# Attention and two gated layers on one core: the second layer's weight sums on VectorE, the sums of its activations earlier and in a block of their own

## The chip, the cores and the metric

One core of a Trainium2 chip runs one program: attention for 2 x 12 heads, then two feed-forward layers with two matrix products each. The metric is the device time of one execution in microseconds. Before the change the median of three runs is 565.75 us (563.14 to 567.88).

## The reference, cut to what matters

```python
attn_out = _attn_ref(q, k, v, cap)          # 2 x 12 heads, 448 tokens, 64 wide; tanh cap, softmax
x = attn_out as (896 tokens, 768)
def _moe_ref(x, w_gate, w_val, w_out, rms_g):   # 768 -> 1536 -> 768
    xn = x / sqrt(mean(x * x) + 1e-6) * rms_g
    g, val = xn @ w_gate, xn @ w_val
    return (silu(g) * val) @ w_out
def _moe2_ref(x, w_in, w_out, alpha):           # 768 -> 2048 -> 768
    h = x @ w_in
    return (maximum(h, 0) + alpha * minimum(h, 0)) @ w_out
```

Everything is float32. The "second layer" of this document is the second product of the first block, the one with `moe_w_out` (1536 to 768).

## The kernel before, in words

After the attention all matrix products are written with seven block products in place of eight (Strassen's scheme in Winograd's form): weights and activations are cut in 2 x 2 blocks, sums and differences of blocks are multiplied, and the products are added up again. The sums of weight blocks are S1 to S4 (S1 = A21 + A22, S2 = S1 - A11, S3 = A22 - S2, S4 = A12 - S2), those of activations T1 to T4. Each float32 operand is split in a high part in the matmul's own format (fp32r), made by a cast on ScalarE, and a low rest, made by a subtraction on VectorE; a product is then three matmuls: high by high, high by low, low by high.

The work is an ordered list of slots. A slot is one product with one weight unit: 18 matmuls of 128x128 weights by 448 columns. `slots` fixes TensorE's order, and `do(n, rank, fn, ...)` hangs a step of another engine behind the matmuls of slot n; the steps of one slot are written in order of rank. Every engine takes its own instructions strictly in the order in which they are written, and waits where an instruction needs another engine's result.

There are four stretches of slots: "g" (gate and value weights, first layer), "o" (`w_out`, 22 slots), "z" (`w_in` of the second block) and the last product. `o0` is the first slot of "o"; slots are counted from it here, so slot -8 is the eighth before it. The products of "o" come in the order P1 (slots 0, 1), P2, the kept part for output row 1 (c11 in the code, 4 and 5), P6 (6, 7), P5 (8, 9), P7, kept part c12, P3, P4, and the kept parts c21 and c22 (18 to 21).

A weight unit (128 x 768 float32) goes through these steps: a load (`w_load`, L101, on the sync queue, started by `w_next` when one of three `raw` buffers has come free), `w_top` (L112, ScalarE), `w_bits` (L117, VectorE; tile `wt`), for sums `w_sum` (L125, GpSimd by default, VectorE where `add` says so), then two slots before its product `w_hi` (L131, ScalarE; tile `wh`) and `w_lo` (L137, VectorE; tile `wl`). The activations of "o" lie in blocks `hb[0]`, `hb[1]` (each four quarters of 2 x 448 columns; `h_quarter(j, h)` is quarter j of half h) and `hb[2]`. `osplit` and `osplit_low` make high and low of one operand (tiles `xx`), `psplit` those of the kept parts, `o_sum` subtracts quarters in place, `t2_sum` makes one difference in tiles of its own. All the elementwise sums are one helper, `tt` (L622, VectorE). `o_copy`, `o_plus`, `keep5`, `plus5` take the results out of PSUM.

In "g", what TensorE accumulates for a group g is read by VectorE between two products on the same PSUM pair: `u3` and `add22` stand behind slot -9 for group 4, and P3 of group 4 in slot -8 goes on to add into the pair that `add22` reads, so it waits for it.

Of the kernel before, what the change touches and what calls it, by code (L numbers as in the profile page):

```python
# [14 lines left out]
ALU = mybir.AluOpType  # L15
# [42 lines left out]
def attn_moe_kernel(ctx: ExitStack, tc: tile.TileContext, units, qk_in, v, sel, w, gvec, alpha, out):  # L58
    nc = tc.nc
# [362 lines left out]
    with tc.manual_schedule():  # L422
# [52 lines left out]
        last = NPAIR - 1  # L475
# [34 lines left out]
        for i in range(NPAIR):  # L510
# [5 lines left out]
            if i:  # L516
                home = {1: (ps_r, "u"), 2: (ps_o, "o")}.get(i)
# [46 lines left out]
        def ct(name):  # L564
            return xpool.tile([P, 2, S], F32, tag="ct", name=name, bufs=2)
# [49 lines left out]
        def block(n, dt=F32):  # L615
            return (xpool if n in (1, 2) else main).tile([P, 8, S], dt, tag=f"b{n}", name=f"b{n}")

        def cu(name):
            return main.tile([P, 2, S], F32, tag="cu", name=name, bufs=2)

        def tt(out, a, b, op):
            nc.vector.tensor_tensor(out=out, in0=a, in1=b, op=op)  # L622
# [48 lines left out]
        def do(n, rank, fn, *a):  # L671
            hooks.setdefault(n, []).append((rank, len(hooks[n]) if n in hooks else 0, fn, a))
# [122 lines left out]
        hb, zt = {}, {}  # L795
# [34 lines left out]
        o0 = at_of["o", "P1", 0]  # L830
# [6 lines left out]
        for u in range(2):  # L837
            f = lambda x: ("o", u, x)
            for n, to, a, b, op, home in (
                (2 * u + 1, "S1", "A21", "A22", ALU.add, "A21"), (u + 3, "S2", "S1", "A11", ALU.subtract, "A11"),  # L840
                (u + 5, "S4", "A12", "S2", ALU.subtract, "A12"), (u + 7, "S3", "A22", "S2", ALU.subtract, "A11"),
            ):
                do(o0 + n, 4, w_sum, f(to), f(a), f(b), op, f(home))
        z0 = at_of["z", 0, "P1"]
        for j, u in enumerate(("z", g, x) for x in ("A11", "A21", "A22", "A12") for g in range(2)):
            convs.append((z0 - 8 + j, u))
# [9 lines left out]
        for u in range(2):  # L856
            f = lambda x: ("f", u, x)
# [122 lines left out]
            )  # L980
            nc.scalar.copy(h_t[u], f_t[u].rearrange("p (k m) -> p k m", m=P))

        t2 = {}

        def h_quarter(j, h):
            return t2[h] if j == 4 else hb[h][:, j:j + 5:4]

        def t2_sum(h):
            t2[h] = ct("t2")
            tt(t2[h], h_quarter(3, h), h_quarter(0, h), ALU.subtract)  # L990

        def osplit(way, p, j, h):
            hs, ls = oops.setdefault(p, ({}, {}))
            hs[h] = oplace(12 * way + h)
            nc.scalar.copy(hs[h], h_quarter(j, h))

        def osplit_low(way, p, j, h):
            hs, ls = oops[p]
            ls[h] = oplace(12 * way + 2 + h)
            tt(ls[h], h_quarter(j, h), hs[h], ALU.subtract)  # L1000

        def o_sum(out, a, b):
            for h in range(2):
                tt(h_quarter(out, h), h_quarter(a, h), h_quarter(b, h), ALU.subtract)

        def psplit(l, u):
            hs, ls = px.setdefault(l, ({}, {}))
# [5 lines left out]
            ls[u] = oplace(6 + 4 * l + u)  # L1013
            tt(ls[u], hb[2][:, 4 * u + l:4 * u + l + 3:2], hs[u], ALU.subtract)

        for way, p, j, hi_at, lo_at in (
            (0, "P1", 0, -5, -4), (1, "P2", 2, -2, -1), (0, "P6", 4, 3, 4), (1, "P5", 0, 4, 5), (0, "P7", 1, 8, 8),
            (1, "P3", 3, 10, 11), (0, "P4", 2, 12, 13),
        ):
            for h in range(2):  # L1020
                do(o0 + hi_at + h, 0.2, osplit, way, p, j, h)
                do(o0 + lo_at + h, 2.2, osplit_low, way, p, j, h)
        for n, *abc in ((-2, 0, 1, 0), (6, 1, 3, 1), (11, 2, 2, 4)):
            do(o0 + n, 3.5, o_sum, *abc)
        for h in range(2):
            do(o0 + 2 + h, 3.5, t2_sum, h)
        for l, n in ((0, 1), (1, 6)):
            for u in range(2):
                do(o0 + n + u, 5, psplit, l, u)
                do(o0 + n + 1 + u, 2.5, psplit_low, l, u)  # L1030

        yf, kept = {}, {}

        def y_of(i, l):
            if i not in yf:
                yf[i] = block(3 - i)
            return yf[i][:, 3 * l:3 * l + 3]

        def o_parts(bank):
            return (ob[bank][0][:, :, :S], slice(0, 2)), (ob[bank][1][:, :1, :S], slice(2, 3))  # L1040

        def o_copy(bank, to):
            for src, c in o_parts(bank):
                nc.scalar.copy(y_of(*to)[:, c], src)

        def o_plus(bank, to):
            for src, c in o_parts(bank):
                tt(y_of(*to)[:, c], src, y_of(*to)[:, c], ALU.add)

        def keep5():  # L1050
            kept[5] = [cu("p5"), cu("p5")]
            for (src, _), t in zip(o_parts(1), (kept[5][0], kept[5][1][:, :1])):
                nc.scalar.copy(t, src)

        def plus5(bank, last):
            for (src, c), t in zip(o_parts(bank), (kept[5][0], kept[5][1][:, :1])):
                tt(y_of(1, 1)[:, c] if last else t, src, t, ALU.add)

        for n, rank, fn, *a in (
            (2, 1, o_copy, 0, (0, 0)), (6, 1, o_plus, 1, (0, 0)), (8, 1, o_copy, 0, (0, 1)), (10, 1, keep5),  # L1060
            (12, 1, plus5, 0, False), (16, 1, o_plus, 1, (0, 1)), (20, 1, o_copy, 0, (1, 0)), (22, 1, plus5, 1, True),
        ):
            do(o0 + n, rank, fn, *a)

# [91 lines left out]
        for k in range(KC):  # L1156
            n = f0 + (-3, -3, -2, -2, 0, 0, 2, 2)[k]
# [171 lines left out]
```

## Time and profile before

| what | value |
|---|---|
| median of the runs | 565.75 us (563.14, 565.75, 567.88) |
| the profiled execution | 564.36 us, span of its instructions 562.6 us |
| mean granted clock of TensorE | 0.997 of full speed |
| TensorE busy | 552.1 us, 98% of the span |
| VectorE busy | 469.8 us, 84% |
| ScalarE busy | 353.9 us, 63% |
| GpSimd busy | 132.7 us, 24% |

Starts and lengths are in microseconds from the first instruction. The length of a VectorE instruction is shown to its end; the next one starts some 0.08 us before that end, so a row of 0.95 takes 0.87 of the queue. In the profile's rows PE is TensorE, DVE VectorE, ACT ScalarE and POOL GpSimd; idle time stands in brackets with what ended it.

### The profile page before, as it was taken

What the parts mean: (1) busy time and instruction counts of PE and PEld (TensorE: products, weight loads), DVE (VectorE), ACT (ScalarE), POOL (GpSimd) and SP (SyncE); (2) the same over time, 40 slices, a digit from 0 to 9 for tenths busy, and PEclk for the clock granted to TensorE, in tenths of its full rate; (3) what the DMA queues carried; (4) which work ended last, traced back from release to release, by engine and by line L of the source; (5) the groups of instructions that cost most, each with busy time, mean ns of one, the idle gap of its engine ahead of it and who ended that gap; (6) DMA issues with size and microseconds to landing.
All of it is one profiled execution on the core that took longest, in us unless ns stands there. A gap on an engine that the chain in (4) does not pass through costs nothing.

```text
span 562.6 us, 7709 instructions
## 1 busy us (share of the span) xinstructions
PE 552.1 (98%) x3057; PEld 462.8 (82%) x3057; DVE 469.8 (84%) x515; ACT 353.9 (63%) x410; POOL 132.7 (24%) x69
## 2 busy tenths in 40 slices
PE   8999999999999999999979999999999999999997
PEld 5444444698999999999868999999999999999996
DVE  4797789899998777689899898969998999999242
ACT  7989999458365463555647554496588996467110
POOL 0025761200155245013190018400461000000000
PEclk9999999999999999999989999999999999999999
DMA  7755420400434434155510475003431347013022
GB/s 264 253 194 187 144 75 3 169 2 0 132 124 149 157 114 168 39 188 168 175 51 0 148 240 175 1 0 119 160 116 57 111 167 256 28 58 113 0 99 98
DMA packets 17180, 66.07 MB, mean 117 GB/s; under 512 B 3448, under 2 KB 5368, under 8 KB 17144
## 3 DMA queue, kind: packets, MB, share of 16 engines
q1 hardware_dynamic: 16712, 65.07, 34.4%
q8 instruction: 24, 0.39, 0.3%
q10 hardware_dynamic: 288, 0.38, 0.2%
q0 software_dynamic: 144, 0.13, 0.1%
q14 instruction: 12, 0.10, 0.0%
HBM read 62.66 MB, written 2.75 MB: 116 GB/s over the span
## 4 chain that ended last, share of the span: by engine, by line
PE 88%; DVE 7%; ACT 2%; DMA 1%; issue 1%; DVEq 0%; ACTq 0%; SPq 0%
PE s L403 21%; PE m L403 19%; PE m L746 10%; PE s L746 9%; PE oo L234 6%; PE s L205 6%; PE s L720 5%; PE m L720 4%; PE us L247 3%; DVE xx L622 2%; DVE wl L137 2%; PE m L416 1%; PE s L416 1%; DVE wt L117 1%; DVE b L622 1%
## 5 line engine op out<-in xcount | busy, mean ns | idle before, releaser
L125 POOL TENSOR_TENSOR wt<-wt 128x768 f32<-128x768 f32 x48 | 109.3, 2286 | 238.9 <-DVE wt L117 131.9
L131 ACT CAST wh<-wt 128x768 fp32r<-128x768 f32 x105 | 87.1, 834 | 82.9 <-PE s L746 24.8
L137 DVE TENSOR_TENSOR wl<-wt,wh 128x768 fp32r<-128x768 f32 x108 | 124.5, 1158 | 7.6 <-ACT wh L131 7.4
L112 ACT CAST top<-raw 128x768 f16<-128x768 bf16 x64 | 68.9, 1079 | 46.4 <-DVE wt L117 30.6
L403 PE MATMUL s<-xx,wh 128*128 128x448 f32 x384 | 92.7, 367 | 0.0
L403 PEld LDWEIGHTS s<-xx,wh 128*128 128x128 f32 x384 | 71.9, 188 | 7.6 <-issue 0.9
L117 DVE SCALAR_TENSOR_TENSOR wt<-raw,top 128x768 uint32<-128x768 uint32 x68 | 68.7, 1012 | 1.4 <-ACT top L112 1.4
L403 PE MATMUL m<-xx,wh 128*128 128x448 f32 x288 | 68.6, 365 | 0.0
L403 PEld LDWEIGHTS m<-xx,wh 128*128 128x128 f32 x288 | 54.1, 188 | 4.3
L622 DVE TENSOR_TENSOR xx<-b,xx 128x896 fp32r<-128x896 f32 (+1 forms) x38 | 50.0, 1322 | 0.6 <-ACT xx L635 0.6
L403 PE MATMUL s<-xx,wl 128*128 128x448 f32 x192 | 49.4, 366 | 0.0
L746 PE MATMUL m<-xx,wh 128*128 128x448 f32 x156 | 47.2, 365 | 0.0
L214 ACT ACTIVATE pt<-s,cinv 128x896 f32<-128x896 f32 (+1 forms) x48 | 41.1, 912 | 6.1 <-PE s L205 5.9
L746 PE MATMUL s<-xx,wh 128*128 128x448 f32 x132 | 40.4, 365 | 0.0
L234 PE MATMUL oo<-pt,vt 128*32 128x448 f32 x384 | 38.6, 540 | 0.5 <-ACT pt L219 0.4
L720 PE MATMUL m<-xx,wh 128*128 128x448 f32 x120 | 35.5, 377 | 3.1 <-DVE xx L622 3.1
L403 PEld LDWEIGHTS s<-xx,wl 128*128 128x128 f32 x192 | 36.1, 188 | 2.9
L403 PE MATMUL m<-xx,wl 128*128 128x448 f32 x144 | 37.0, 365 | 0.0
L219 ACT ACTIVATE pt<-pt,cap_t 128x3136 f32<-128x3136 f32 (+2 forms) x13 | 35.3, 2714 | 0.4
L622 DVE TENSOR_TENSOR b<-m,b 128x896 f32<-128x896 f32 (+1 forms) x17 | 16.6, 977 | 21.8 <-PE m L746 18.1
L234 PEld LDWEIGHTS oo<-pt,vt 128*32 128x32 f32 x384 | 12.1, 110 | 23.8 <-issue 21.0
L746 PEld LDWEIGHTS m<-xx,wh 128*128 128x128 f32 x156 | 29.3, 188 | 2.3
(193 smaller groups left out, 1006.5 us busy)
## 6 DMA issues: line engine op xcount, KB each, us to landing
raw<-w_in SPq DMA_DIRECT2D x68, 768.0 KB
rw<-qk_in SPq DMA_DIRECT2D x11, 480.0 KB
vt<-v_in SPq DMA_DIRECT2D x12, 256.0 KB
out<-b SPq DMA_DIRECT2D x2, 448.0 KB
out<-b SPq DMA_DIRECT2D x2, 224.0 KB
out<-e SPq DMA_DIRECT2D x1, 448.0 KB
out<-c SPq DMA_DIRECT2D x2, 224.0 KB
gt<-us SPq DMA_DIRECT2D x22, 3.5 KB
```

The costliest lines, as they stand in the source:

```text
L112: copy(top_of[u].bitcast(F16)[:, 1::2], raw_t[u].bitcast(BF16)[:, 4:4 * n + 4:4])
L117: nc.vector.scalar_tensor_tensor(out=f_t[u].bitcast(U32), in0=raw_t.pop(u).bitcast(U32)[:, 1:2 * n + 1:2], scalar=13, in1=top_of.pop(u), o ...
L125: add(out=t, in0=f_t[a], in1=f_t[b], op=op)
L131: copy(h_t[u], f_t[u].rearrange("p (k m) -> p k m", m=P))
L137: nc.vector.tensor_tensor(out=l_t[u], in0=f_t[u].rearrange("p (k m) -> p k m", m=P), in1=h_t[u], op=ALU.subtract)
L214: nc.scalar.activation(out=t[:, 2 * g:2 * g + w], in_=st.pop((i, g))[:, :w, :S], func=AF.Tanh, scale=cinv)
L219: nc.scalar.activation(out=t[:, done:to], in_=t[:, done:to], func=AF.Exp, scale=cap_t)
L234: nc.tensor.matmul(oo[i][q * Q:q * Q + Q, :S], vv[:, n, q % 2 * Q:q % 2 * Q + Q], t[:, min(n, TILES - 1), :], start=c == 0, stop=c == TG, ...
L403: nc.tensor.matmul(ps[:, r, :S], lhs, rhs, start=first and n == 0, stop=n == len(mm) - 1, skip_group_check=True,)
L622: nc.vector.tensor_tensor(out=out, in0=a, in1=b, op=op)
L720: nc.tensor.matmul(dst[m], wt[:, kk * MB + m, :], x, start=first and u == 0 and kk == 0 and n == 0, stop=u == 1 and kk == 1 and n == 2, sk ...
L746: nc.tensor.matmul(dst[m], wt[:, kk * MB + m, :], x, start=start and ks + kk == 0 and i == 0, stop=fin and last and kk == 1 and i == 2, sk ...
```

## The change

Three things change, all in the second layer ("o"):

- The eight sums of its weights (S1 to S4, for two units) go from GpSimd to VectorE, at other slots: S1 behind slots 0 and 3, S2 behind 1 and 3, S3 behind 7 and 8, S4 behind 9 and 10.
- Six of the eight differences of its activations (T1, T2 and T3 for two halves) are made behind slots -16 to -10, three times one for the first half and three for the second. T1 and T2 go to a free block (`y_block(0)`, quarters 4 and 5 of `h_quarter`) instead of in place and in tiles of their own. The last two (T4) stand behind slots 9 and 10.
- As that block is also that of the layer's output, results are kept in other tiles first (`o_keep`, a copy on ScalarE) and added later (`o_join`, on VectorE), at the slots of the copies and sums before. The low parts of P5's two halves both stand behind slot 5, and those of the kept parts' second half behind 9 and 10 instead of 7 and 8.

```diff
-                (2 * u + 1, "S1", "A21", "A22", ALU.add, "A21"), (u + 3, "S2", "S1", "A11", ALU.subtract, "A11"),
...
+                (3 * u, "S1", "A21", "A22", ALU.add, "A21"), (2 * u + 1, "S2", "S1", "A11", ALU.subtract, "A11"),
...
-                do(o0 + n, 4, w_sum, f(to), f(a), f(b), op, f(home))
+                do(o0 + n, 4, w_sum, f(to), f(a), f(b), op, f(home), nc.vector.tensor_tensor)
...
+        def y_block(i):
+            if i not in yf:
+                yf[i] = block(3 - i)
+            return yf[i]
+
         def h_quarter(j, h):
-            return t2[h] if j == 4 else hb[h][:, j:j + 5:4]
-
-        def t2_sum(h):
-            t2[h] = ct("t2")
-            tt(t2[h], h_quarter(3, h), h_quarter(0, h), ALU.subtract)
+            if j > 3:
+                return y_block(0)[:, 4 * (j - 4) + 2 * h:4 * (j - 4) + 2 * h + 2]
+            return hb[h][:, j:j + 5:4]
...
-        def o_sum(out, a, b):
-            for h in range(2):
-                tt(h_quarter(out, h), h_quarter(a, h), h_quarter(b, h), ALU.subtract)
+        def o_sum(h, out, a, b):
+            tt(h_quarter(out, h), h_quarter(a, h), h_quarter(b, h), ALU.subtract)
...
-        for n, *abc in ((-2, 0, 1, 0), (6, 1, 3, 1), (11, 2, 2, 4)):
+        for n, *abc in ((-16, 0, 4, 1, 0), (-15, 0, 5, 3, 4), (-14, 0, 1, 3, 1), (-12, 1, 4, 1, 0), (-11, 1, 5, 3, 4),
+                        (-10, 1, 1, 3, 1), (9, 0, 2, 2, 5), (10, 1, 2, 2, 5)):
             do(o0 + n, 3.5, o_sum, *abc)
-        for h in range(2):
-            do(o0 + 2 + h, 3.5, t2_sum, h)
...
-        def o_plus(bank, to):
-            for src, c in o_parts(bank):
-                tt(y_of(*to)[:, c], src, y_of(*to)[:, c], ALU.add)
...
+        def o_keep(p, bank):
+            tile = ct if p == "U2" else cu
+            kept[p] = tile("p"), tile("p")[:, :1]
+            for (src, _), t in zip(o_parts(bank), kept[p]):
                 nc.scalar.copy(t, src)
 
+        def o_join(p, bank, to=None):
+            for (src, c), t in zip(o_parts(bank), kept[p]):
+                tt(y_of(*to)[:, c] if to else t, src, t, ALU.add)
```

In the rows below `b_1761` is `hb[1]`, `b_1384` is `hb[0]`, `b_1993` the free block, and `c_` are the partial results of the first layer. VectorE behind slots -12 to -9, before (the last two rows are `u3` and `add22` of group 4):

```order
L117 SCALAR_TENSOR_TENSOR wt<-raw,top_93 128x768
L622 TENSOR_TENSOR c_2135<-m,c_2016 128x896
L137 TENSOR_TENSOR wl<-wt,wh 128x768
L622 TENSOR_TENSOR b_1761<-c_1816,b_1761 128x448
L137 TENSOR_TENSOR wl<-wt,wh 128x768
L622 TENSOR_TENSOR b_2161<-s,b_2161 128x448
L622 TENSOR_TENSOR c_2188<-m,c_2016 128x896
L622 TENSOR_TENSOR c_2188<-s,c_2188 128x896
```

And VectorE at the same place after the change:

```order
L117 SCALAR_TENSOR_TENSOR wt<-raw,top_93 128x768
L622 TENSOR_TENSOR b_1993<-b_1761 128x896
L622 TENSOR_TENSOR c_2140<-m,c_2018 128x896
L137 TENSOR_TENSOR wl<-wt,wh 128x768
L622 TENSOR_TENSOR b_1993<-b_1761,b_1993 128x896
L622 TENSOR_TENSOR b_1761<-c_1816,b_1761 128x448
L137 TENSOR_TENSOR wl<-wt,wh 128x768
L622 TENSOR_TENSOR b_1761<-b_1761 128x2x448
L622 TENSOR_TENSOR b_2167<-s,b_2167 128x448
L622 TENSOR_TENSOR c_2195<-m,c_2018 128x896
L622 TENSOR_TENSOR c_2195<-s,c_2195 128x896
```

Three differences of the second half now stand between the same eight instructions, all of them ahead of `u3` and `add22`.

VectorE behind slots 2 to 5 of the second layer, before (`ks` and the `xx` of L137 are low parts of kept weights; `t_2537` and `t_2568` are the two halves of T2, and the `xx` made from them the low parts of P6's operand):

```order
L117 SCALAR_TENSOR_TENSOR wt<-raw,top_93 128x768
L622 TENSOR_TENSOR t_2537<-b_1384 128x896
L137 TENSOR_TENSOR ks<-wt,ks 128x768
L622 TENSOR_TENSOR xx<-b_2161,xx 128x896
L117 SCALAR_TENSOR_TENSOR wt<-raw,top_94 128x768
L622 TENSOR_TENSOR t_2568<-b_1761 128x896
L137 TENSOR_TENSOR wl<-wt,wh 128x768
L622 TENSOR_TENSOR xx<-t_2537,xx 128x896
L137 TENSOR_TENSOR wl<-wt,wh 128x768
L622 TENSOR_TENSOR xx<-t_2568,xx 128x896
L622 TENSOR_TENSOR xx<-b_1384,xx 128x896
```

And after the change:

```order
L117 SCALAR_TENSOR_TENSOR wt<-raw,top_93 128x768
L137 TENSOR_TENSOR ks<-wt,ks 128x768
L622 TENSOR_TENSOR xx<-b_2167,xx 128x896
L117 SCALAR_TENSOR_TENSOR wt<-raw,top_94 128x768
L125 TENSOR_TENSOR wt<-wt 128x768 x2
L137 TENSOR_TENSOR wl<-wt,wh 128x768
L622 TENSOR_TENSOR xx<-b_1993,xx 128x896
L137 TENSOR_TENSOR wl<-wt,wh 128x768
L622 TENSOR_TENSOR xx<-b_1993,xx 128x896 x3
```

The two sums of T2 have gone, and S1 and S2 of the second weight unit (L125) stand there instead; the last row holds both halves of P6's and P5's low parts but the first.

## Rows read from the trace of the kernel before

**Rows 1.** The page's first part: busy time, share, instructions.
```profile
PE 552.1 (98%) x3057; PEld 462.8 (82%) x3057; DVE 469.8 (84%) x515; ACT 353.9 (63%) x410; POOL 132.7 (24%) x69
```
**Rows 2.** Timeline of TensorE, second layer: start, length, what, idle before it.
```profile
258.63 0.57 PE L720 MATMUL m<-xx,wh 128*128 128x448 f32 x2
...
278.59 3.71 PE L720 MATMUL s<-xx,ks 128*128 128x448 f32 x17 [1.16 <-DVE xx L622]
...
285.60 0.47 PE L720 MATMUL m<-xx,wh 128*128 128x448 f32 x1 [3.10 <-DVE xx L622]
...
294.51 0.65 PE L720 MATMUL s<-xx,wh 128*128 128x448 f32 x2
295.94 0.48 PE L720 MATMUL s<-xx,wl 128*128 128x448 f32 x1 [0.78 <-DVE wl L137]
```
**Rows 3.** The chain in order of time, where the second layer ends: start, length, what.
```profile
347.10 7.29 PE m L403 x36
```
**Rows 4.** Busy time in stretches: PE, PEld, DVE, ACT, POOL, granted clock, DMA.
```profile
286.70:290.00 3.30, 3.30 (x10) 2.94 (x10) 3.30 (x2) 2.76 (x4) 3.30 (x3) 0.50 0.00 0
```
**Rows 5.** Timeline of VectorE, second layer.
```profile
255.12 2.09 DVE L622 TENSOR_TENSOR b<-b 128x896 f32<-128x896 f32 x2
...
262.93 1.85 DVE L137 TENSOR_TENSOR wl<-wt,wh 128x768 fp32r<-128x768 f32 x1
...
279.32 1.08 DVE L622 TENSOR_TENSOR t<-b 128x896 f32<-128x896 f32 x1
280.32 2.62 DVE L137 TENSOR_TENSOR wl<-wt,wh 128x768 fp32r<-128x768 f32 x1
282.86 2.68 DVE L622 TENSOR_TENSOR xx<-t,xx 128x896 fp32r<-128x896 f32 x1
...
290.63 2.73 DVE L622 TENSOR_TENSOR xx<-b,xx 128x896 fp32r<-128x896 f32 x1
...
295.81 1.08 DVE L622 TENSOR_TENSOR xx<-b,xx 128x896 fp32r<-128x896 f32 x1
```
**Rows 6.** Timeline of GpSimd, end of the first layer and second layer.
```profile
218.49 1.85 POOL L125 TENSOR_TENSOR wt<-wt 128x768 f32<-128x768 f32 x1 [4.46 <-DVE wt L117]
221.30 4.62 POOL L125 TENSOR_TENSOR wt<-wt 128x768 f32<-128x768 f32 x2 [0.96 <-DVE wl L137]
...
279.48 15.59 POOL L125 TENSOR_TENSOR wt<-wt 128x768 f32<-128x768 f32 x6 [13.00 <-DVE wt L117]
```
**Rows 7.** Groups of VectorE: its weight sums in the last product.
```profile
L125 DVE TENSOR_TENSOR wt<-wt 128x768 f32<-128x768 f32 x8 | 7.6, 954 | 0.0
```
**Rows 8.** The chain in order of time, second layer.
```profile
268.36 4.24 DMA raw<-w_in
...
276.57 0.04 DVE ks L137
```
**Rows 9.** Groups of VectorE from 200 to 231.8 us: busy, mean ns, idle before.
```profile
L622 DVE TENSOR_TENSOR c<-m,c 128x896 f32<-128x896 f32 x6 | 6.6, 1092 | 7.1 <-PE m L403 7.1
```
**Rows 10.** Timeline of VectorE, slots -12 to -9 of the first layer.
```profile
217.46 0.95 DVE L117 SCALAR_TENSOR_TENSOR wt<-raw,top 128x768 uint32<-128x768 uint32 x1
218.70 1.09 DVE L622 TENSOR_TENSOR c<-m,c 128x896 f32<-128x896 f32 x1 [0.29 <-PE m L403]
219.71 1.45 DVE L137 TENSOR_TENSOR wl<-wt,wh 128x768 fp32r<-128x768 f32 x1
221.08 0.61 DVE L622 TENSOR_TENSOR b<-c,b 128x448 f32<-128x448 f32 x1
221.62 2.60 DVE L137 TENSOR_TENSOR wl<-wt,wh 128x768 fp32r<-128x768 f32 x1
...
226.00 1.09 DVE L622 TENSOR_TENSOR c<-m,c 128x896 f32<-128x896 f32 x1 [1.25 <-PE m L403]
227.12 1.09 DVE L622 TENSOR_TENSOR c<-s,c 128x896 f32<-128x896 f32 x1
```
**Rows 11.** Timeline of TensorE: slot -8 (P3 of group 4) starts.
```profile
229.45 0.77 PE L403 MATMUL s<-xh,wh 128*128 128x448 f32 x3
```

More of the change, by code (lines that the diff above doesn't have):

```diff
@@ L839, in attn_moe_kernel @@
             for n, to, a, b, op, home in (
-                (2 * u + 1, "S1", "A21", "A22", ALU.add, "A21"), (u + 3, "S2", "S1", "A11", ALU.subtract, "A11"),
-                (u + 5, "S4", "A12", "S2", ALU.subtract, "A12"), (u + 7, "S3", "A22", "S2", ALU.subtract, "A11"),
+                (3 * u, "S1", "A21", "A22", ALU.add, "A21"), (2 * u + 1, "S2", "S1", "A11", ALU.subtract, "A11"),
+                (u + 7, "S3", "A22", "S2", ALU.subtract, "A21"), (u + 9, "S4", "A12", "S2", ALU.subtract, "A12"),
             ):
-                do(o0 + n, 4, w_sum, f(to), f(a), f(b), op, f(home))
+                do(o0 + n, 4, w_sum, f(to), f(a), f(b), op, f(home), nc.vector.tensor_tensor)
         z0 = at_of["z", 0, "P1"]
@@ L981, in w_kept @@
             nc.scalar.copy(h_t[u], f_t[u].rearrange("p (k m) -> p k m", m=P))
-        t2 = {}
+        yf, kept = {}, {}
+        def y_block(i):
+            if i not in yf:
+                yf[i] = block(3 - i)
+            return yf[i]
         def h_quarter(j, h):
-            return t2[h] if j == 4 else hb[h][:, j:j + 5:4]
-        def t2_sum(h):
-            t2[h] = ct("t2")
-            tt(t2[h], h_quarter(3, h), h_quarter(0, h), ALU.subtract)
+            if j > 3:
+                return y_block(0)[:, 4 * (j - 4) + 2 * h:4 * (j - 4) + 2 * h + 2]
+            return hb[h][:, j:j + 5:4]
         def osplit(way, p, j, h):
@@ L1014, in psplit_low @@
             tt(ls[u], hb[2][:, 4 * u + l:4 * u + l + 3:2], hs[u], ALU.subtract)
-        for way, p, j, hi_at, lo_at in (
-            (0, "P1", 0, -5, -4), (1, "P2", 2, -2, -1), (0, "P6", 4, 3, 4), (1, "P5", 0, 4, 5), (0, "P7", 1, 8, 8),
-            (1, "P3", 3, 10, 11), (0, "P4", 2, 12, 13),
+        for way, p, j, hi_at, lo_at, step in (
+            (0, "P1", 0, -5, -4, 1), (1, "P2", 2, -2, -1, 1), (0, "P6", 5, 3, 4, 1), (1, "P5", 4, 4, 5, 0),
+            (0, "P7", 1, 8, 8, 1), (1, "P3", 3, 10, 11, 1), (0, "P4", 2, 12, 13, 1),
         ):
             for h in range(2):
-                do(o0 + hi_at + h, 0.2, osplit, way, p, j, h)
-                do(o0 + lo_at + h, 2.2, osplit_low, way, p, j, h)
-        for n, *abc in ((-2, 0, 1, 0), (6, 1, 3, 1), (11, 2, 2, 4)):
+                do(o0 + hi_at + step * h, 0.2, osplit, way, p, j, h)
+                do(o0 + lo_at + step * h, 2.2, osplit_low, way, p, j, h)
+        for n, *abc in ((-16, 0, 4, 1, 0), (-15, 0, 5, 3, 4), (-14, 0, 1, 3, 1), (-12, 1, 4, 1, 0), (-11, 1, 5, 3, 4),
+                        (-10, 1, 1, 3, 1), (9, 0, 2, 2, 5), (10, 1, 2, 2, 5)):
             do(o0 + n, 3.5, o_sum, *abc)
-        for h in range(2):
-            do(o0 + 2 + h, 3.5, t2_sum, h)
-        for l, n in ((0, 1), (1, 6)):
+        for l, n, n_low in ((0, 1, 2), (1, 6, 9)):
             for u in range(2):
                 do(o0 + n + u, 5, psplit, l, u)
-                do(o0 + n + 1 + u, 2.5, psplit_low, l, u)
-        yf, kept = {}, {}
+                do(o0 + n_low + u, 2.5, psplit_low, l, u)
         def y_of(i, l):
-            if i not in yf:
-                yf[i] = block(3 - i)
-            return yf[i][:, 3 * l:3 * l + 3]
+            c = 5 if (i, l) == (0, 1) else 3 * l
+            return y_block(i)[:, c:c + 3]
         def o_parts(bank):
@@ L1044, in o_copy @@
                 nc.scalar.copy(y_of(*to)[:, c], src)
-        def o_plus(bank, to):
-            for src, c in o_parts(bank):
-                tt(y_of(*to)[:, c], src, y_of(*to)[:, c], ALU.add)
-        def keep5():
-            kept[5] = [cu("p5"), cu("p5")]
-            for (src, _), t in zip(o_parts(1), (kept[5][0], kept[5][1][:, :1])):
+        def o_keep(p, bank):
+            tile = ct if p == "U2" else cu
+            kept[p] = tile("p"), tile("p")[:, :1]
+            for (src, _), t in zip(o_parts(bank), kept[p]):
                 nc.scalar.copy(t, src)
-        def plus5(bank, last):
-            for (src, c), t in zip(o_parts(bank), (kept[5][0], kept[5][1][:, :1])):
-                tt(y_of(1, 1)[:, c] if last else t, src, t, ALU.add)
+        def o_join(p, bank, to=None):
+            for (src, c), t in zip(o_parts(bank), kept[p]):
+                tt(y_of(*to)[:, c] if to else t, src, t, ALU.add)
         for n, rank, fn, *a in (
-            (2, 1, o_copy, 0, (0, 0)), (6, 1, o_plus, 1, (0, 0)), (8, 1, o_copy, 0, (0, 1)), (10, 1, keep5),
-            (12, 1, plus5, 0, False), (16, 1, o_plus, 1, (0, 1)), (20, 1, o_copy, 0, (1, 0)), (22, 1, plus5, 1, True),
+            (2, 1, o_keep, "P1", 0), (6, 1, o_join, "P1", 1, (0, 0)), (8, 1, o_keep, "U2", 0), (10, 1, o_keep, "P5", 1),
+            (12, 1, o_join, "P5", 0), (16, 1, o_join, "U2", 1, (0, 1)), (20, 1, o_copy, 0, (1, 0)),
+            (22, 1, o_join, "P5", 1, (1, 1)),
         ):
```

## The prediction

> **What bounds the kernel now.** First the page: TensorE is busy 98% of the span [rows 1], so the change can win only where TensorE stops. Next its timeline in the second layer [rows 2]: three waits, 1.16, 3.10 and 0.78 us, all ended by VectorE, all at low parts (of a kept part's operand, of P6's operand, of P5's weights). The layer's first matmul stands at 258.63 [rows 2] and the first of the next stretch at 347.10 [rows 3]: 88.5 us. At full rate a slot is 18 x 7.29 / 36 = 3.65 us [rows 3], 22 slots are 80.2. So the layer loses **8.2 us**: 5.0 in the waits; 1.8 between 285.60 and 294.51, where 35 matmuls took 8.9 instead of 7.1 [rows 2], since after the longest wait the granted clock stood at 0.50 (1.2 GHz) from 286.7 to 290 [rows 4]; the rest, 1.4, in restarts and short gaps.
>
> Why VectorE is late shows in its own timeline beside GpSimd's [rows 5, 6]. A low part of weights takes 0.95, one of activations 1.08 (295.81) when GpSimd rests. While GpSimd makes its sums, the same instructions take 2.62, 2.68, 2.73: 1.65 more each, seven of them, from 262.93 (1.85) to 290.63 (2.73), together 6 x 1.65 + 1.0 = 10.9 us. GpSimd pays likewise: 15.59 / 6 = 2.6 a sum instead of 1.85. It is turn by turn: each VectorE instruction with both inputs in SBUF waits out the sum that is running, and GpSimd's next sum waits for that instruction. An instruction that reads PSUM is not held: the one at 218.70 takes its 1.09 in the middle of a sum [rows 6, 10].
>
> **The second layer after the change.** I lay VectorE's queue end to end from 255.12 to the end of P6's first low part. In queue time (0.08 less than shown) a 768-wide instruction costs 0.87, an 896-wide 1.0, a 448-wide 0.54 [rows 5, 7, 10]. Now there are 15 of 0.87 (four are weight sums; on VectorE these show 0.954 [rows 7]), 7 of 1.0 and 4 of 0.54: 22.2 us. The same sum for before has two differences in place (2.09 [rows 5]) and two for T2 more, four weight sums less: 22.7, plus 5.9 for four instructions held by GpSimd (1.0 + 3 x 1.65), plus 1.6 of idle; that is 30.2, and the trace has 285.50 - 255.12 = 30.4 [rows 5], so the method holds. After the change nothing on GpSimd runs beside it, and I allow 1.2 of idle: 278.5. TensorE wants it at slot 6, 258.63 + 6 x 3.65 = 280.5: **2 us to spare** where it was 3 late.
>
> The other two waits: the first hung on a load that landed at 272.6 (268.36 + 4.24) and reached VectorE by way of ScalarE at 276.57 [rows 8]. The load is started when VectorE frees a buffer; without the two differences at 255.12 and without the two held instructions behind 262.93 that step ends near 264.0 instead of 268.3, the load lands near 268.3, the low parts are done near 274.2, and slot 5 begins at 276.9. P5's weights follow P6's second low part (280.7), the sum out of PSUM and one low part: 285, wanted at 287.8. The sums S3 and S4, 4 x 0.87 in slots 7 to 10, and T4's two differences come after that with three slots before P7 wants the first of them: hidden by that lead, and worth 0.87 each if it is gone. ScalarE copies as much as before, `o_join` adds as much as `o_plus` and `plus5`, and the kept parts' late low parts (slots 9, 10) are wanted at slot 12: nothing. GpSimd gets some 20 us free; nobody waits for it there. I take the whole 8.2 back; the bounds are 8.2 (no wait left) and 5.8 (a late load leaves 2.4, below).
>
> **The first layer: a new wait.** Six differences of 1.0 go into VectorE's queue in slots -16 to -10. From 200 to 231.8 VectorE idles 7.1 us in front of six reads of PSUM [rows 9]. The three of the first half fall where GpSimd rests and fit into that idle. The three of the second half don't, because GpSimd has three sums there [rows 6]. Queued behind them are `u3` and `add22`, and P3 of group 4 waits for `add22`: it starts at 229.45 [rows 11], and `add22` now ends at 228.13 (227.12 + 1.01 [rows 10]). There are **1.3 us** to spare. End to end from 218.33 (217.46 + 0.87 [rows 10]):
> - First difference to 219.33. It starts at once, 0.16 before GpSimd could (218.49); the trace has just this at 279.32, where a difference keeps its 1.08 and GpSimd's first sum waits [rows 5, 6]. GpSimd's S1 then runs to 221.1.
> - Read of PSUM to 220.3, not held. Low part: waits for GpSimd, 222.0. Second difference 223.0; S2 on GpSimd waits for it and ends at 224.8.
> - Multiply (448 wide) held until then: 225.35; S3 on GpSimd to 227.15. Low part, held: 228.0. Third difference 229.0. Multiply out of PSUM 229.55; `u3` 230.6; `add22` **231.6**.
>
> TensorE then waits 231.6 - 229.45, with the signal **2.2 us**. Before, the same sums held only two of these instructions (1.45 and 2.60 [rows 10]) and VectorE still idled 1.25 at 226.00; the third sum ran in that idle. Bounds: if GpSimd held nothing, the queue is at 225.2 before `u3`, and there is no wait (0); if all three sums were paid in full, 225.2 + 5.4 + 2.0 = 232.6, a wait of 3.2. I take 2.2, the turns that the rows show. Behind it everything moves alike, and VectorE has caught up by its next read of PSUM.
>
> The Trainium skill (SBUF — State Buffer, "Who interferes with whom") says that such an instruction of VectorE and one of GpSimd hold the shared interface for their whole length and that the order of issue decides which of them is blocked. Taken alone it lets VectorE, whose instructions follow each other without a gap, always be first, and the sum would then be 8.2 with no new wait. The rows disagree on the order: GpSimd gets its turn after every single instruction of VectorE.
>
> **The clock after that wait.** It stayed full after 1.16 and 0.78 and fell after 3.10 [rows 2, 4]; 2.2 lies between. A drop cost 1.8. Bounds 0 and 1.8; I take half, 0.9, since it may differ from one execution to the next.
>
> **Sum.** -8.2 + 2.2 + 0.9 = -5.1 against the profiled execution's 564.36: 559.3. That execution lies 1.4 below the median of the runs, 565.75, so the median to expect is **560.7**, 0.9% less. The runs of before spread over 0.8%, so a measurement of this kernel tells about 1% from no change.
>
> **Rivals.**
> - *No new wait.* GpSimd gives way in slots -12 to -9. For it: VectorE has no gap there, and GpSimd's sums are not wanted at once. Against it: the strict turns of rows 5 and 6. Then -8.2: 557.6 on the median.
> - *The load stays late.* If it lands at 272.6 as before, VectorE gets to `ks` at 276.6; 0.87 + 1.0 is 1.6 late for slot 5, and the five instructions behind it (4.5) end at 282.9, 0.8 late for the shifted slot 6: 2.4 stay, -8.2 + 2.4 + 3.1 = -2.7: 563.0. Against it: each load waits only for a buffer that VectorE frees, and that comes earlier.
> - *Slower.* The long instructions of rows 5 are long by themselves and not because of GpSimd. Then VectorE gets nothing back: 30.4 - 4.0 + 3.5 = 29.9 to P6's low part, still late by all but 0.5; S3 and S4 add 3.5 to a queue that is late, and the first layer's wait comes on top: -0.5 + 3.5 + 3.1 = +6.1, 571.9. It decides from the point where such an instruction in slots 4 to 8 still takes over 2 us with GpSimd idle. For it: the wide ones stand close together in one stretch. Against it: their starts and ends fit GpSimd's, and at 295.81 the same form takes 1.08.
>
> **How the numbers follow.** Forecast 0.60 (559.7 without the clock's drop, 561.5 with it), no new wait 0.15, late load 0.19, slower 0.06. The range 557.0 to 565.0 holds the first three and their scatter and leaves out the slower case. Below 560.1 (over 1% faster) lie the no-wait case and some 0.25 of the forecast's 0.60: 0.40. Slower by over 1% is the slower case, 0.06; within 1% the rest, 0.54.
>
> **What would show it.** In the changed kernel's profile: no wait of TensorE over 0.5 between slots 0 and 22, which then take 80 to 81 us; 128x768 and 128x896 instructions of VectorE in slots 4 to 8 at 0.95 and 1.08; `add22` of group 4 ending 2 us after P3 could start, with a wait of TensorE ended by it; GpSimd busy some 20 us less. I am wrong if there is no wait at slot -8, if the second layer still waits, or if another stretch, above all the start of the "z" slots, waits now that TensorE arrives earlier.

## The result and the profile after

The changed kernel took 559.49 us (median of four runs, 558.98 to 560.76), the kernel before beside it 566.38 (563.14 to 567.88): a ratio of 0.989, 95% interval 0.984 to 0.994. The forecast was 560.7. The profiled execution took 560.76, its span 559.0; before they were 564.36 and 562.6.

The page's first part, after (before in [rows 1]):

```profile
PE 551.5 (99%) x3057; PEld 461.2 (83%) x3057; DVE 466.9 (84%) x523; ACT 353.8 (63%) x410; POOL 112.9 (20%) x61
```

GpSimd is busy 19.8 us less, the forecast's "some 20". TensorE, after: its timeline (the only wait over 0.5 us outside the start, and the second layer's first matmul), then the chain (two slots are 36 matmuls) where that layer ends.

```profile
231.01 0.85 PE L403 MATMUL s<-xh,wh 128*128 128x448 f32 x3 [1.86 <-DVE c L622]
...
260.83 0.57 PE L720 MATMUL m<-xx,wh 128*128 128x448 f32 x2
```

```profile
342.83 7.44 PE m L403 x36
```

The three waits of [rows 2] are gone, and the new wait is where it was forecast, at slot -8: 1.86 us for `add22`, where 2.2 was said. The second layer takes 342.83 - 260.83 = 82.0 us without any wait; 88.5 before. The forecast had 80.3, and the chain says why: 7.44 for 36 matmuls, against 7.29 in [rows 3]. More on that below.

VectorE in slots 4 to 8, after (before in [rows 5]):

```profile
274.15 0.96 DVE L137 TENSOR_TENSOR ks<-wt,ks 128x768 fp32r<-128x768 f32 x1 [0.97 <-ACT ks L981]
...
277.01 1.95 DVE L125 TENSOR_TENSOR wt<-wt 128x768 f32<-128x768 f32 x2
278.88 0.95 DVE L137 TENSOR_TENSOR wl<-wt,wh 128x768 fp32r<-128x768 f32 x1
279.75 1.08 DVE L622 TENSOR_TENSOR xx<-b,xx 128x896 fp32r<-128x896 f32 x1
280.75 0.95 DVE L137 TENSOR_TENSOR wl<-wt,wh 128x768 fp32r<-128x768 f32 x1
281.62 3.09 DVE L622 TENSOR_TENSOR xx<-b,xx 128x896 fp32r<-128x896 f32 x3
```

Every form is back at 0.95 and 1.08 (3.09 for three, with ends that overlap). `ks` starts at 274.15 (276.57 in [rows 8]), so the load did come earlier. P6's first low part is there at 280.8, and slot 6 begins at 260.83 + 6 x 3.72 = 283.2: 2.4 us to spare, where the forecast had 2 (at 3.65 a slot it would be 1.9; the slower pace gives the rest).

VectorE and then GpSimd at slots -12 to -9, after (before in [rows 10, 6]):

```profile
217.87 1.08 DVE L622 TENSOR_TENSOR b<-b 128x896 f32<-128x896 f32 x1
218.87 1.08 DVE L622 TENSOR_TENSOR c<-m,c 128x896 f32<-128x896 f32 x1
219.88 1.61 DVE L137 TENSOR_TENSOR wl<-wt,wh 128x768 fp32r<-128x768 f32 x1
221.41 1.08 DVE L622 TENSOR_TENSOR b<-b,b 128x896 f32<-128x896 f32 x1
222.41 2.26 DVE L622 TENSOR_TENSOR b<-c,b 128x448 f32<-128x448 f32 x1
224.60 2.60 DVE L137 TENSOR_TENSOR wl<-wt,wh 128x768 fp32r<-128x768 f32 x1
227.13 1.08 DVE L622 TENSOR_TENSOR b<-b 128x896 f32<-128x896 f32 x1
...
229.77 1.09 DVE L622 TENSOR_TENSOR c<-s,c 128x896 f32<-128x896 f32 x1
```

```profile
218.03 2.64 POOL L125 TENSOR_TENSOR wt<-wt 128x768 f32<-128x768 f32 x1 [3.46 <-DVE wt L117]
221.63 4.76 POOL L125 TENSOR_TENSOR wt<-wt 128x768 f32<-128x768 f32 x2 [0.96 <-DVE wl L137]
```

One reads the turns from starts and ends: the difference at 217.87 keeps its 1.08 and the sum at 218.03 takes 2.64; the low part at 219.88 waits that sum out (1.61); the difference at 221.41 keeps its 1.08 and the second sum waits; then the 448-wide multiply (2.26, alone 0.61) and the low part (2.60) each wait out one sum. `add22` (229.77) ends at 230.86, and TensorE goes on at 231.01. The L117 ahead of the first row starts at 217.00, in [rows 10] at 217.46. This trace is 0.46 earlier here, and 0.44 of that stands already at 108 us, ahead of the change; the two are compared below with 0.46 added.

The stretch behind that wait, in the order of [rows 4]: the granted clock stayed full.

```profile
231.50:235.00 3.50, 3.50 (x18) 3.18 (x17) 1.64 (x4) 2.47 (x3) 0.00 (x0) 1.00 0.02 5
```

### The profile page after: what moved, and what is told of

Read it like the earlier page. It is cut to its first block, busy times and chain, and to the rows that moved or that the text cites. A ratio compares the mean times of both kernels' runs of the same rounds, so it can differ in the third digit from the quotient of the medians.

```text
span 559.0 us, 7703 instructions
## 1 busy us (share of the span) xinstructions
PE 551.5 (99%) x3057; PEld 461.2 (83%) x3057; DVE 466.9 (84%) x523; ACT 353.8 (63%) x410; POOL 112.9 (20%) x61
## 4 chain that ended last, share of the span: by engine, by line
PE 94%; DVE 4%; ACT 1%; issue 0%; DVEq 0%
PE s L403 22%; PE m L403 18%; PE m L746 10%; PE s L746 9%; PE s L720 8%; PE m L720 7%; PE oo L234 6%; PE s L205 5%; PE us L247 3%; PE m L416 1%; PE s L416 1%; DVE b L622 1%; DVE wl L137 1%; DVE c L622 1%; ACT pt L219 1%; PE us L257 1%
## 5 line engine op out<-in xcount | busy, mean ns | idle before, releaser
L125 POOL TENSOR_TENSOR wt<-wt 128x768 f32<-128x768 f32 x40 | 89.5, 2243 | 255.6 <-DVE wt L117 144.4
L137 DVE TENSOR_TENSOR wl<-wt,wh 128x768 fp32r<-128x768 f32 x108 | 120.7, 1123 | 11.0 <-ACT wh L131 10.8
L117 DVE SCALAR_TENSOR_TENSOR wt<-raw,top 128x768 uint32<-128x768 uint32 x68 | 68.6, 1011 | 0.9 <-ACT top L112 0.9
L622 DVE TENSOR_TENSOR xx<-b,xx 128x896 fp32r<-128x896 f32 (+1 forms) x40 | 47.0, 1183 | 0.6 <-ACT xx L635 0.6
```

Of the source, the lines that this page charges most:

```text
L117: nc.vector.scalar_tensor_tensor(out=f_t[u].bitcast(U32), in0=raw_t.pop(u).bitcast(U32)[:, 1:2 * n + 1:2], scalar=13, in1=top_of.pop(u), o ...
L125: add(out=t, in0=f_t[a], in1=f_t[b], op=op)
L137: nc.vector.tensor_tensor(out=l_t[u], in0=f_t[u].rearrange("p (k m) -> p k m", m=P), in1=h_t[u], op=ALU.subtract)
```

## The experiments

Medians stand beside runs of the kernel before on the same chip; where one time is given, it is that of one profiled execution. Line numbers in rows are each kernel's own. In the first batch (e1 to e4) before took 565.28 (25 runs), in the second (e5 to e8) 564.00 (17), in the third (e9 to e11) 565.09 (15).

**e1: the changed kernel again.** No edit.

> The changed kernel once more, nothing edited. The profiled execution had a wait of TensorE of 1.86 us at slot -8 and behind it, from 231 to 384 us, matmuls 206.7 ns apart instead of 202.6 (7.44 us for 36 instead of 7.30), some 3 us in all. If that slower pace is a matter of chance at the restart, this trace may show the other pace or another stretch; if it comes with the wait by rule, it begins again at 231. Time near 559.5 either way; wait at slot -8 again 1.7 to 2.2.

Measured: 561.32 (12 runs, 558.25 to 565.46), ratio 0.993 (0.990 to 0.996). The profiled execution took 559.28. The timeline of TensorE, then the stretch behind the wait:

```profile
230.75 1.01 PE L403 MATMUL s<-xh,wh 128*128 128x448 f32 x3 [1.86 <-DVE c L622]
...
261.57 0.57 PE L720 MATMUL m<-xx,wh 128*128 128x448 f32 x2
```

```profile
231.50:235.00 3.50, 3.50 (x11) 3.11 (x11) 1.38 (x2) 2.21 (x3) 0.00 (x0) 0.54 0.02 5
```

And where the layer ends, in the chain:

```profile
230.75 12.75 PE s L403 x54
...
342.00 7.30 PE m L403 x36
```

The wait is the same 1.86, but here the granted clock fell to 0.54 in that stretch (the 1.2 GHz level for nearly all of it): 54 matmuls took 12.75 where 54 x 7.30 / 36 = 10.95 is full rate, 1.8 us. The second layer is 342.00 - 261.57 = 80.4 us (forecast 80.3), at 7.30 a pair of slots, and no row behind the wait runs at 7.44: the slower pace does not come with the wait by rule. The median is 1.8 above the 559.5 that was expected.

**e2: the second half's three differences later,** where GpSimd makes no such row of sums.

```diff
-        for n, *abc in ((-16, 0, 4, 1, 0), (-15, 0, 5, 3, 4), (-14, 0, 1, 3, 1), (-12, 1, 4, 1, 0), (-11, 1, 5, 3, 4),
-                        (-10, 1, 1, 3, 1), (9, 0, 2, 2, 5), (10, 1, 2, 2, 5)):
+        for n, *abc in ((-16, 0, 4, 1, 0), (-15, 0, 5, 3, 4), (-14, 0, 1, 3, 1), (-8, 1, 4, 1, 0), (-7, 1, 5, 3, 4),
+                        (-5, 1, 1, 3, 1), (9, 0, 2, 2, 5), (10, 1, 2, 2, 5)):
```

> The second half's three differences at slots -8, -7 and -5 instead of -12, -11 and -10, where GpSimd rests and VectorE idles 1.9, 0.9 and 2.4 us. Turn-by-turn theory: the wait at slot -8 goes, the second layer stays free of waits, 1.9 us less than the changed kernel, and 3 more if the slower pace came from that wait: 554.5 to 557.7. Rival (the six differences are too much for VectorE anywhere in the first layer): a wait of 1 us or more shows at another slot, and the time stays at 559.5.

Measured: 556.68 (6 runs, 556.03 to 559.98), ratio 0.986 (0.983 to 0.989). TensorE waits nowhere over 0.3 us from slot -16 on. VectorE's `u3` and `add22`, and where TensorE's second layer begins and ends (timelines, and the chain for the end):

```profile
226.13 1.09 DVE L622 TENSOR_TENSOR c<-m,c 128x896 f32<-128x896 f32 x1 [1.25 <-PE m L403]
227.26 1.09 DVE L622 TENSOR_TENSOR c<-s,c 128x896 f32<-128x896 f32 x1
```

```profile
258.76 0.57 PE L720 MATMUL m<-xx,wh 128*128 128x448 f32 x2
```

```profile
339.18 7.30 PE m L403 x36
```

The idle time of 1.25 ahead of `u3` is back as in [rows 10], and the layer still takes only 80.4. So the place of three differences among GpSimd's sums made the wait at slot -8, and nothing else of the change needs it; e5 takes the sums away instead.

**e3: the weight sums alone.** The kernel before with its eight sums on VectorE at the new slots; differences as before. The lines left out are the slots, as in the change's own diff.

```diff
...
-                do(o0 + n, 4, w_sum, f(to), f(a), f(b), op, f(home))
+                do(o0 + n, 4, w_sum, f(to), f(a), f(b), op, f(home), nc.vector.tensor_tensor)
```

> The kernel before with the weight sums alone on VectorE at their new slots; differences of activations where they were. Turn-by-turn theory: no VectorE instruction of the second layer is held any more, but the four differences (4.0 us) are still in the queue to P6's low part: 278.5 + 4 = 282.5 against slot 6 at 280.5, a wait of 1.5 to 2.5 there, none at slot -8; 5 to 6 less than before, 560 to 561.5. Rival (the early differences are what helps): within 1.5 us of before, since four sums of 0.87 take the place of the differences.

Measured: 558.63 (6 runs, 557.65 to 562.64), ratio 0.989 (0.986 to 0.993). TensorE's timeline (the second layer's start and its two waits), and the layer's end in the chain:

```profile
258.24 0.57 PE L720 MATMUL m<-xx,wh 128*128 128x448 f32 x2
...
281.46 0.47 PE L720 MATMUL m<-xx,wh 128*128 128x448 f32 x1 [0.96 <-DVE xx L622]
...
300.20 0.47 PE L720 MATMUL m<-xx,wh 128*128 128x448 f32 x1 [0.25 <-DVE xx L622]
```

```profile
340.39 7.29 PE m L403 x36
```

The layer takes 82.15: of the 8.2 us to be had, 6.3 come from the sums alone, more than I had expected of them. Two waits are left, 1.2 together, and no wait at slot -8.

**e4: the early differences alone.** The changed kernel with its weight sums back on GpSimd, at the old slots (e3's edit in reverse).

> The changed kernel with the weight sums back on GpSimd at their old slots; differences stay early. Turn-by-turn theory: seven instructions of VectorE at 2.6 to 2.7 again; to P6's low part 22.2 - 3.5 + 5.9 + 1.6 = 26.2, so 0.5 to 1.5 late at slot 6, more behind it as all of P6's and P5's low parts are held; with the wait at slot -8 some 3 to 5 less than before, 561.5 to 563.5. Rival (early differences are what helps): as fast as the changed kernel, 559.5.

Measured: 569.45 (10 runs, 566.96 to 570.83), ratio 1.006 (1.0035 to 1.009): slower than before, with an interval above 1, where I had expected a gain. TensorE's waits, VectorE's low parts of P6 and P5, and GpSimd's sums beside them (timelines):

```profile
291.35 0.47 PE L720 MATMUL m<-xx,wh 128*128 128x448 f32 x1 [2.79 <-DVE xx L622]
...
297.73 0.64 PE L720 MATMUL s<-xx,wh 128*128 128x448 f32 x2 [2.67 <-DVE b L622]
```

```profile
288.60 7.99 DVE L622 TENSOR_TENSOR xx<-b,xx 128x896 fp32r<-128x896 f32 x3
296.51 1.61 DVE L622 TENSOR_TENSOR b<-s,p 128x896 f32<-128x896 f32 x2
```

```profile
280.92 14.72 POOL L125 TENSOR_TENSOR wt<-wt 128x768 f32<-128x768 f32 x6 [12.97 <-DVE wt L117]
```

Three low parts take 7.99 in place of 3.09, since GpSimd is in the middle of six sums. Behind them stands the sum out of PSUM at 296.51 (`o_join` of P1), and P5 waits for that too: 2.67 us that nothing had before. My expectation had left it out: the two low parts of P5 now stand ahead of it, behind slot 5. It named no fall of the clock either, and there were two, worth 1.9 each: behind the wait at slot -8 (granted 0.59 from 230.8 to 235; 36 matmuls in 9.19, at full rate 7.30) and behind these waits (0.75 from 297.7 to 302; 34 in 8.79, at full rate 6.90).

**e5: group 5's weight sums on VectorE.** These are the sums of GpSimd in slots -12 to -9; the rest is the changed kernel.

```diff
+    def adder(lay, g):
+        return nc.vector.tensor_tensor if (lay, g) == ("g", 5) else nc.gpsimd.tensor_tensor
...
-        w_sum((lay, g, "S1"), (lay, g, "A21"), (lay, g, "A22"), ALU.add)
+        w_sum((lay, g, "S1"), (lay, g, "A21"), (lay, g, "A22"), ALU.add, add=adder(lay, g))
...
```

> The changed kernel with the three weight sums of the first layer's group 5 (S1, S2, S3; the sums that GpSimd makes in slots -12 to -9) on VectorE instead of GpSimd. Turn by turn: no VectorE instruction there is held, each keeps 0.95 or 1.08, VectorE pays 3 x 0.87 = 2.6 for the sums themselves; add22 of group 4 ends near 229.9 (225.2 + 2.6, u3 and add22 2.0 and their read), so the wait of TensorE at slot -8 falls from 1.9 to at most 0.4 and the clock stays full after it: 557 to 559 us, 1 to 2 below the changed kernel. Rival, the order of the differences alone makes the wait and GpSimd has no part in it: the sums come on top of a queue that is late already, the wait grows to over 3 and the time to 561 or more.

Measured: 561.96 (10 runs, 559.41 to 563.58), ratio 0.995 (0.993 to 0.997). The wait in TensorE's timeline:

```profile
229.85 0.83 PE L406 MATMUL s<-xh,wh 128*128 128x448 f32 x3 [0.49 <-DVE c L625]
```

And the two instructions of VectorE that GpSimd held for 2.26 and 2.60:

```profile
223.68 0.62 DVE L625 TENSOR_TENSOR b<-c,b 128x448 f32<-128x448 f32 x1
224.22 0.95 DVE L137 TENSOR_TENSOR wl<-wt,wh 128x768 fp32r<-128x768 f32 x1
```

The wait did as the turns say (0.49; at most 0.4 expected): three more instructions on VectorE make it shorter, because none is held. The time did not: 562 where 557 to 559 was expected. e9 and e10 look for the reason.

**e6: needless sums on GpSimd.** The changed kernel with seven sums on GpSimd into a tile that nobody reads.

```diff
+        def idle_sums(u, k):
...
+            a = f_t["o", u, "A22"].rearrange("p (h m) -> p h m", h=2)
+            for _ in range(k):
+                nc.gpsimd.tensor_tensor(out=idle[0], in0=a, in1=a, op=ALU.add)
+
+        do(o0, 4.5, idle_sums, 0, 2)
+        do(o0 + 3, 3.5, idle_sums, 1, 5)
```

> The changed kernel with seven sums on GpSimd that nobody reads (half of one weight unit, 128x768, added to itself, into a tile of its own): two behind slot 0 and five behind slot 3 of the second layer. VectorE's instructions and their order are untouched. Turn by turn: low parts of VectorE in slots 4 to 7 are held 1.65 us each again and show 2.6 to 2.7 in place of 0.95 and 1.08, five of them, 8.3 us; with 2 us to spare TensorE waits about 6 us for P6's low part at slot 6, the clock falls after it (1.8): 566 to 568 us. Rival, such an instruction of VectorE is long only by its own place in the queue and not by GpSimd: all keep 0.95 and 1.08, no wait in the second layer, 559 to 561.5 us.

Measured, one execution: 568.13. GpSimd's needless sums, VectorE's low parts beside them, TensorE's wait (timelines), and the stretch behind it:

```profile
279.04 10.86 POOL L851 TENSOR_TENSOR idle<-wt 128x768 f32<-128x768 f32 x5 [12.99 <-DVE wt L117]
```

```profile
281.96 2.22 DVE L137 TENSOR_TENSOR wl<-wt,wh 128x768 fp32r<-128x768 f32 x1
284.10 2.35 DVE L622 TENSOR_TENSOR xx<-b,xx 128x896 fp32r<-128x896 f32 x1
```

```profile
286.50 0.74 PE L720 MATMUL m<-xx,wh 128*128 128x448 f32 x1 [3.58 <-DVE xx L622]
```

```profile
286.00:290.00 4.00, 3.50 (x9) 3.15 (x10) 4.00 (x3) 0.04 (x1) 3.83 (x2) 0.50 0.02 4
```

This shows the cause: VectorE's instructions and their order are the same as after, and 0.95 becomes 2.22 by GpSimd alone. Each was held 1.27, less than the 1.65 of the sums before, so the wait is 3.6 and not 6. A needless sum is shorter by as much: the first, which nothing holds, takes 1.47 where [rows 6] have 1.85. And the fall of the clock follows it as it did in [rows 4].

**e7 and e8: e2 and e3 again,** side by side.

> The same kernel as e2 (the second half's three differences behind slots -8, -7 and -5 instead of -12, -11 and -10), beside the next one on one chip. If the early differences and their block are worth something where they meet no sum of GpSimd: 556.5 to 557.5 us, and 1.5 to 2.5 below the next kernel, which has three waits of 1.2, 2.0 and 1.0 in the second layer where this one has none. If moving them is worth nothing: both within 0.8 us of each other.

> The same kernel as e3 (the kernel before with the eight weight sums on VectorE at their new slots, the differences of the activations as before), beside the kernel before this one in the list. If its three waits of 1.2, 2.0 and 1.0 us in the second layer cost what they last, less what restarts take in: 558 to 559.5 us. If they are made up elsewhere (a later wait for the same data): 556.5 to 557.5 like the other.

(Both texts misread e3's row of waits: 1.2 was the total of two, 1.0 the longer of them.) Measured: 558.48 (6 runs, 555.60 to 560.57) and 560.43 (6 runs, 557.01 to 562.49); ratios 0.9885 (0.985 to 0.992) and 0.991 (0.988 to 0.994). The difference of the two is 1.95, and it was 1.95 in the first batch. With six runs each, which scatter over 5 us, that alone is weak, and the traces bear out only part of it. In the first batch the layer takes 82.15 - 80.4 = 1.75 more without the early differences. In this batch's two executions it takes 82.0 in e7 and 81.6 in e8. The layer's start in e7's timeline and its end in the chain, then the same of e8:

```profile
260.55 0.57 PE L720 MATMUL m<-xx,wh 128*128 128x448 f32 x2
...
342.55 7.44 PE m L403 x36
```

```profile
260.22 0.57 PE L720 MATMUL m<-xx,wh 128*128 128x448 f32 x2
...
341.83 7.30 PE m L403 x36
```

All of e7's layer and the first six slots of e8's ran at the slower pace of 7.44. Taken off, they are 80.5 and 81.2, 0.7 apart: TensorE comes later to slot 6 at that pace, and the only wait that e8's trace shows in the layer is 0.24. So the early differences, where they meet no sum, are worth 1.75 at the faster pace and 0.7 in this pair; that both batches give 1.95 is chance in part. Both medians lie 1.8 above those of the first batch, though.

**e9 and e10: e5 again,** for two more profiles.

> The same kernel as e5 (group 5's weight sums on VectorE), for a second profile. Its wait had fallen from 1.9 to 0.49 and its profiled execution took 559.4, yet most of its executions took 562. Theory of the matmul pace: its waits are the same again (0.5 at slot -8, none in the second layer), and whatever the execution takes above 556 is the stretch in which 36 matmuls take 7.44 in place of 7.30 (2% of that stretch; an execution of 562 would show some 290 us of it). Rival, a wait that the first profile did not have: the execution shows a wait of 1 us or more in the chain and 7.30 nearly throughout.

> The same kernel as e5 and e9, a third profile, as in some executions the stretch at 7.44 should stand elsewhere: same waits, and the time again 556 plus 2% of the stretch at 7.44 us per 36 matmuls, within 0.7 us.

Measured: 560.72 and 556.53, with waits of 0.2 and 0.5 at slot -8 and none in the second layer. So no hidden wait; what differs is the pace of the matmuls. First e9's chain at one place in the first layer, then the same place in e10's:

```profile
178.11 7.44 PE m L406 x36
```

```profile
177.99 7.30 PE m L406 x36
```

And one long stretch of both, e9 (PE and clock alone) and then e10 (columns as in [rows 4]), neither with a wait in it:

```profile
390.00:540.00 150.00, 150.00 (x728) 1.00 0.29 100
```

```profile
390.00:540.00 150.00, 150.00 (x742) 138.92 (x741) 126.66 (x130) 95.41 (x121) 13.71 (x6) 1.00 0.30 104
```

In the same 150 us, at a granted clock of 1.00, TensorE does 728 matmuls or 742, 1.9% more: 206.7 or 202.7 ns each (7.44 and 7.30 by 36). A stretch of such slots that lasts T is longer by T x 0.14 / 7.44 when it runs at the slower pace. Taken off, the executions of e5, e9 and e10 agree at 556.0 to 556.8:

| profiled execution | time | us at 7.44 | longer by | time less that |
|---|---|---|---|---|
| before | 564.36 | 26 | 0.5 | 563.9 |
| after | 560.76 | 182 | 3.4 | 557.3 |
| e1 (after again) | 559.28 | 0 | 0 | 559.3, with 1.8 of clock |
| e2, e7 (differences later) | 559.81, 560.47 | 197, 234 | 3.7, 4.4 | 556.1, 556.1 |
| e3, e8 (weight sums alone) | 557.65, 562.49 | 26, 301 | 0.5, 5.7 | 557.2, 556.8 |
| e5, e9, e10 (group 5) | 559.52, 560.72, 556.53 | 167, 208, 26 | 3.1, 3.9, 0.5 | 556.4, 556.8, 556.0 |
| e11 (both) | 559.63 | 197 | 3.7 | 555.9 |

The stretches are summed from the chain's rows of 17 matmuls or more after 105 us. The slots right behind the wait at slot -8 count where single matmuls show the pace (slow in the changed kernel, fast in e5, e9 and e10); e4 and e6 are left out, with their longer waits. The last column is worked out, not measured, and what sets the pace is open: that e5's median of 562 comes from longer slow stretches fits its three profiles, of which none was at 562.

**e11: e2 and e5 together.**

> e2 and e5 together: the second half's differences behind slots -8, -7 and -5, and group 5's weight sums on VectorE. By waits: e2 had none left from the first layer to the end, so taking GpSimd's turns away gives nothing more, and three sums on VectorE are hidden: the same as e2 on the same chip within 1 us, 556.5 to 559 us with its pace. Rival, VectorE becomes late behind slots -12 to -5 with 2.6 us of sums and 3 us of differences more: a wait of 1 us or more at slot -8 to -4, 559.5 us or more. A pace of 7.44 in the profiled execution adds 2% of its stretch and speaks for neither.

Measured: 559.40 (10 runs, 555.83 to 563.67), ratio 0.991 (0.988 to 0.994). TensorE has no wait from slot -16 on, as in e2, and nothing is gained over it, as the first theory said: 555.9 in the table against 556.1. The median itself is 0.4 above the range expected.

## Why the prediction was right, point by point

- **The second layer gives 8.2 back: right in mechanism and size.** 88.5 became 80.4 in e1, and 82.0 in the profiled execution of the changed kernel, which is the same 22 slots at 7.44. The three waits went for the reasons given: instructions at 0.95 and 1.08 where GpSimd rests, an earlier `ks`, 2 us to spare at slot 6. e6 shows the reason alone: with GpSimd set to work again, 0.95 became 2.22 and a wait of 3.6 came back. What the working had not done was to share the 8.2 out. At the faster pace e3 gives 6.3 of it to the weight sums, and the moved differences the other 1.8; e4 shows that the differences without the sums make things worse. (By its own rows the working's 10.9 is 10.8, as 1.85 is 0.9 over 0.95, and its 8.2 is 8.3; neither moves the forecast.)
- **A new wait of 2.2 at slot -8: right, a little too large.** The idle time is 1.86, in three other runs of the same order 1.86 or 1.87. The forecast counted from start to start, though: slot -8 begins at 231.01, or 231.47 with the 0.46 added, against 229.45, so the like of 2.2 is 2.0. The turns came in the order that was laid out, from the first difference ahead of GpSimd's first sum on: the first low part ended at 221.41 + 0.46 = 221.9, where 222.0 was said. What was too long is the hold: the working let the 448-wide multiply and the second low part each wait out a whole sum from its start, some 1.8, and they were held 1.65 (2.26 and 2.60 in place of 0.61 and 0.95), as the rows of the second layer had shown. In e5, where GpSimd holds nothing there, the wait is 0.49, with three sums more in VectorE's queue.
- **The clock after that wait, half of 1.8: a mean that no execution showed.** Of four profiled executions with this wait, the clock fell in two (e1 and e4) and stayed full in two (the changed kernel and e6). Four fit a half and do not prove it, and the length of a wait alone did not decide: the clock also stayed at 1.00 after the 2.79 of e4.
- **The sum.** Without a fall of the clock the working gave -8.2 + 2.2 = -6.0; the profiled executions differ by -6.6 once the slow pace is taken off (563.9 to 557.3), of which 0.46 came ahead of the change; -6.1 is left. As they stand they differ by only -3.6, since the changed kernel's ran 182 us at 7.44 and before's 26. The median moved by -6.9 here and by -4.0 in e1's batch; the pace makes such a difference between batches, and the forecast's -5.1 lies between. That the number came out only 1.2 off is thus luck in part: a difference of 2.9 us of pace, which the working did not know of, could have moved it either way.
- **The rivals.** "No new wait" fell with the 1.86. "The load stays late" fell with `ks` at 274.15. "Slower" fell with 0.95 and 1.08 in slots 4 to 8, and by its mechanism with e6.
- **The turns.** The Trainium skill (SBUF — State Buffer, "Who interferes with whom") lets the order of issue decide which engine is blocked. The prediction took that to mean that VectorE, without gaps, would always be first, and said that the rows disagree. They agree, once it is read for one instruction at a time: GpSimd's second sum stands waiting from 221.63, ahead of the multiply that starts at 222.41, and runs first; the multiply stands waiting before the third sum starts (ScalarE reads the second's result at 224.22), and runs next; the third sum is ahead of the low part of 224.60. The turns come out of that rule, and the forecast, which went by the turns of the rows, did not need its own reading of it.

What the change is worth is so the work taken off GpSimd. The six early differences, as the change places them, bring nothing on top: at most 1.8 gained in the second layer, 2.0 lost at slot -8, and 1.8 more by the clock in two of the four profiles. With the pace taken off, the weight sums alone come to 557.2 and 556.8 (e3 and e8), the changed kernel to 557.3; the medians of the first batch are 558.63 for e3 and 561.32 for e1. Put where GpSimd rests (e2), the differences keep their gain without the loss: 556.1, and the fastest median of both batches.

## What to carry to other kernels

Where VectorE's instructions come out at more than twice their length, look at GpSimd's timeline beside them before anything else: work taken off GpSimd, even onto the late VectorE itself, can make VectorE earlier. A step moved out of a crowded stretch must be laid into the queue it goes to together with the other engine's work there; three differences of 1.0 cost no wait at slots -8 to -5 and made a wait at -12 to -10. And before two medians 1% apart are explained by the schedule, compare the matmul pace of the same slots in both traces.

## What the runs showed of the hardware that was not expected

TensorE has two paces for the same matmuls at a granted clock of 1.00, 202.7 and 206.7 ns for 128 x 448, uniform for tens to hundreds of microseconds. One kernel shows both in different executions, and one execution both in turn. Most changes stand at one of a few places of the program where TensorE stops for 0.04 to 0.2 us, a stop that no wait of the views explains in full. Such a stop is not enough for a change. One place is a group of six matmuls near 383 in e7, where the pace goes from slow to fast (1.28 from start to start at 382.69, where 1.24 is the slow pace); the same group in the kernel before stops for longer (1.58 at 386.46, six of the faster pace take 1.38), and the pace there is the faster one on both sides. TensorE's timelines of e7 and of before:

```profile
382.69 1.44 PE L403 MATMUL s<-xx,wh 128*128 128x448 f32 x6
383.97 0.78 PE L403 MATMUL s<-xx,wl 128*128 128x448 f32 x3
384.58 1.38 PE L403 MATMUL s<-xx,wh 128*128 128x448 f32 x6
385.80 0.77 PE L403 MATMUL s<-xx,wl 128*128 128x448 f32 x3
```

```profile
386.46 1.58 PE L403 MATMUL s<-xx,wh 128*128 128x448 f32 x6
```

Six matmuls take 1.40 at the slower pace and 1.38 at the faster. After the new wait at slot -8 either pace could follow: 7.44 in the changed kernel, 7.30 in e1. At 412.7 in e5 it changed with no stop to be seen. What decides it was not tried.
